# Part of an exponential moved to accumulating DMAs, more of it off ScalarE, and one chunk split in two

## The chip, the cores and the metric

The kernel runs on one core of one Trainium2 chip. A core has five engines that run their own instruction streams and meet through semaphores: TensorE (matrix products, into the eight banks of PSUM), ScalarE (activations), VectorE (elementwise work and reductions), GpSimd, and SyncE, which issues DMAs. GpSimd can issue DMAs too. The metric is device time in microseconds of one execution, as the median of several.

## What is computed

One transformer layer with layer norm ahead of each half, on 2048 rows of 640 columns in bfloat16: attention with 32 heads of 20 columns, then a gated feed-forward of width 1728.

```python
h  = x  + softmax(q k^T * 20**-0.5) v @ wo      # q, k, v = split(layernorm(x) @ wqkv), 32 heads of 20
h2 = h  + (gelu(layernorm(h) @ w_gate) * (layernorm(h) @ w_up)) @ w_down
```

The softmax needs 32 x 2048 x 2048 exponentials, 1,048,576 for each of the 128 partitions. That is the bulk of the work.

## The kernel before

**Tiles, quads, slots, chunks.** Scores are made transposed: a tile is one PSUM bank of 128 keys by 512 columns for one head (where a chunk has 256 queries, the 512 columns are two blocks of keys, with 128 queries four). Four heads are multiplied at once in four row groups of TensorE; a quad is the four tiles of one group of four heads. The queries are cut into chunks (`SIZES`, L316), and each chunk into slots of 64 tiles (16 quads), so that there are 32 slots in all, 2048 tiles. Softmax needs no maximum: a bound for each query is subtracted through an extra row of the product.

**Two ways to the exponential.** Most tiles go through ScalarE: one ACTIVATE takes two or three neighbouring banks and writes bfloat16 into `pts` or `pts2` (18 tiles of room). `D_QUADS` (L334) says how many of a slot's 16 quads go through VectorE instead (`d_exp`, L862 to 902). There each tile is read out of PSUM as scaled int16 (L881), a bit trick that leaves exponent and fraction in one integer; after two tiles (narrow, slots 0 to 17) or four (wide, from slot `D_WIDE` = 18 on) seven instructions in all follow on the whole group: fraction bits out (L892), a linear term (L893), its square (L894), times the fraction (L895), the addition of this correction onto the integer (L896), and a last scaling (L897) after which the bits are the bfloat16 result. (L894 to 896 have two tensor operands, the others one.) `dv0`, `dv` and `dvw` are the buffers of these groups, `df` and `dw` their scratch.

**PSUM patterns.** `PAT` (L818) gives a unit its banks: three and two in turn, or, in the slots of `SIX`, three and three, where a VectorE tile takes the third bank of a unit. The other banks (`BG`, L1210) serve the background: projections, output product, feed-forward. Bank 6 collects the product with v for one slot; its end is the copy to `osb` in `epilogue` (L1029).

**Where the VectorE tiles are placed.** `dq` (L813) gives each a place among ScalarE's tiles: spread over its slot, `D_LEAD` tiles ahead of it; where the lead is 0, the spread is pressed into the first `D_PART` of the slot. The product with v for a VectorE quad is taken up at least `D_LAG` units after its last tile was computed (L1009).

**What sets the order.** A planner (`Sched.schedule`, L94) places all operations by priority, readiness and free banks, with a duration and a latency for each, written in the code; `emit` then writes each engine's instructions in the planned order, with semaphore waits. An engine runs its own list strictly in order. So what the planner took for the time of an operation decides only the order, and an operation that is later than planned holds up all behind it on its engine.

**After a chunk.** `post` (L1065) takes the rows of a finished chunk from `o_nat` through transposes, the product with wo, the residual, the layer norm (`ln_apply`, into `xn_t`, L1101), transposes again (by DMA from SyncE, except in the tail), and the feed-forward as background work (`mms`, L1114; the casts L1155, the gelu pass L1161 on ScalarE with an activation table change on either side, the products L1169; `down`, L1185). `BASE` tells which of four row blocks of `h_sb`, `o_nat`, `hnT` and `ha_f` a chunk uses; a later chunk with the same block waits until the earlier one has left it. `prefetch` (L1055) loads the residual rows. For chunks before the last, the reciprocal root of the layer norm runs on GpSimd (L557 to 590).

Of the kernel before, what the change touches and what calls it, by code (L numbers as in the profile page):

```python
# [7 lines left out]
ALU = mybir.AluOpType  # L8
# [299 lines left out]
D = 640  # L308
# [7 lines left out]
SIZES = (512, 512, 256, 256, 256, 128, 128)  # L316
BASE = (0, 0, 0, 2, 0, 2, 3)
SIX = tuple(range(8, 16))
# [12 lines left out]
D_LAG = 9  # L331
MERGE = ()
PR, PR2 = 12, 6
D_QUADS = (1,) + (2,) * 15 + (2, 2) + (3, 2) * 5 + (2, 2, 2, 2)  # L334
D_FIRST, D_PART = 2, 0.75
D_LEAD = ((0,) * 8, (0, 10, 20) + (24,) * 21)
# [8 lines left out]
def bass_sequential_preLN__mha_block__glu_gated_geglu__prompt_kernel(  # L345
# [12 lines left out]
    with ExitStack() as es:  # L358
# [22 lines left out]
        sel = sb("sel", [128, NA, H])  # L381
        zer = sb("zer", [128, 32])
        sel0 = sb("sel0", [128, 4, 32])
# [17 lines left out]
        osb = sb("osb", [128, 2, 512], FP32)  # L401
        rc = sb("rc", [128, 2, 16], FP32)
        o_nat = sb("o_nat", [128, 4, D])
        sq = sb("sq", [128, 512])
        xn_t = sb("xn_t", [128, 2, D])
        dvx = sb("dvx", [128, 1024])
# [23 lines left out]
        aq = [carve(512) for _ in range(2)] + [sq[:], xn_t[:, 0, 0:512], xn_t[:, 1, 0:512]]  # L430
# [26 lines left out]
        dw1 = carve(1024).bitcast(F16)  # L457
        carve = carver(qt_all[:, 0, :, :].rearrange("p g s -> p (g s)"), NG * 512)
        dvw += [carve(2048).bitcast(I16) for _ in range(2)]
        dv.append(dvx[:].bitcast(I16))  # L460
        zb = dvx[:].rearrange("p (i s) -> p i s", i=2)
        dv0 = [ha_f[:, 1024 * i:1024 * i + 1024].bitcast(I16) for i in range(5)]
        df0, dw0 = ha_f[:, 5120:6144], ha_f[:, 6144:7168].bitcast(F16)
        carve = carver(qt_all[:, 1, :, :].rearrange("p g s -> p (g s)"), NG * 512)
        df2 = carve(2048)
        dw2 = carve(2048).bitcast(F16)
# [42 lines left out]
        cst(I("memset", sel[:], -1.0), "sel", 160)  # L509
        cst(I("affine_select", out=sel[:], in_=sel[:], compare_op=ALU.is_ge, fill=0.0, base=0,  # L510
              pattern=[[128, NA], [-DH, H]], channel_multiplier=1), "sel", 160)
        cst(I("affine_select", out=sel[:], in_=sel[:], compare_op=ALU.is_ge, fill=0.0, base=DH - 1,
              pattern=[[-128, NA], [DH, H]], channel_multiplier=-1), "sel", 160)
        cst(I("memset", sel0[:], 0.0), "sel0")
# [77 lines left out]
        def ln_apply(eng, src, dst, dkey, t, rkeys, prio, first=False):  # L592
            if eng == "act":
                fn = I("activation", dst, src, ACT.Identity, bias=nm[:, t:t + 1], scale=rs[:, t:t + 1])
            else:
# [3 lines left out]
                      reads=list(rkeys) + [("mu", t), ("rs", t)] + ([("nm", t)] if eng == "act" else []), writes=[dkey])  # L599
# [68 lines left out]
        def aqk(t):  # L668
            return ("xn", t - 3) if t >= 3 else ("aq", t)
# [99 lines left out]
        def q_bound0(banks, prio):  # L769
# [3 lines left out]
                bank(bk), sel0[:].rearrange("p j e -> p (j e)"), aq[0], start=True, stop=True),  # L773
# [77 lines left out]
        d_cur = [None]  # L851
        d_late = []
# [9 lines left out]
        def d_exp(b, tile, prio, u):  # L862
# [5 lines left out]
            if h == 0:  # L868
                busy = set(x[1][1] for x in d_done)
                pool = [(kind, i) for i in range(5 if kind != "w" or CHUNKS[slots[units[u][0][0]][0]][0] >= 1536 else 3)]  # L870
                pool = [p for p in pool if p not in busy]
                assert pool
                d_cur[0] = min(pool, key=lambda p: d_last.get(p, -1))
                d_last[d_cur[0]] = len(d_ops)
# [3 lines left out]
            keys = [("dv", i)] + ([("dv", ("l", k)) for k in ((0, 1), (2, 3), ())[i[1]]] if kind == "w" and i[1] < 3 else [])  # L878
            aft = tuple(e_ops) + (q_done(0) if c else ()) + (q_done(1) + tuple(d_late) if kind == "w" else ()) + \
                (q_done(2) if kind == "w" and i[1] > 2 else ())  # L880
# [8 lines left out]
            zi = df.bitcast(I16)  # L889
            w_ = len(d_raw) / 2  # L890
            d = lambda fn, n, r, w: d_ops.append(op("dve", fn, 0.066 + n * w_, prio, reads=r, writes=w))
            d(I("tensor_scalar", zi, v, 511, 2048, ALU.bitwise_and, ALU.bitwise_or), 0.265, [("dv", i)], ["df"])  # L892
            d(I("tensor_scalar", dw, zi, CA / OCT, CB, ALU.mult, ALU.add), 0.265, ["df"], ["dw"])  # L893
            d(I("tensor_tensor", dw, dw, dw, ALU.mult), 0.53, ["dw"], ["dw"])  # L894
            d(I("tensor_tensor", dw, dw, zi, ALU.mult), 0.53, ["df", "dw"], ["dw"])  # L895
            d(I("tensor_tensor", v, v, dw, ALU.add), 0.53, ["dw", ("dv", i)], [("dv", i)])  # L896
# [127 lines left out]
        def epilogue(s_, bk, d_sums):  # L1024
# [4 lines left out]
            op("dve", I("tensor_copy", osb[:, s, :], PS[:, 512 * 6:512 * 7]), c_dve(512), P_QK,  # L1029
               reads=[("O", s_)], writes=[("osb", s)], rel=[bk], after=tuple(d_sums))  # L1030
# [7 lines left out]
            for tt in range(4):  # L1038
                op("pe", lambda eng, tt=tt: eng.transpose(bank(b2)[:, tt * 128:(tt + 1) * 128],
                                                          osb[:, s, tt * 128:(tt + 1) * 128], identf[:]),  # L1040
# [255 lines left out]
```

## Time and profile before

| | |
|---|---|
| runs | 915.77, 915.27, 914.54 us (median 915.27) |
| profiled execution | 916.19 us, span 914.2 us |
| ScalarE busy | 881.1 us (96%) |
| TensorE busy | 824.1 us (90%) |
| VectorE busy | 794.1 us (87%) |
| GpSimd busy | 48.2 us (5%) |
| DMA | 34.33 MB, mean 38 GB/s |

The span is cut where the profiler saw the first and last instruction; the execution's own time is 2.0 us longer. PE is TensorE, PEld its weight loads, DVE VectorE, ACT ScalarE, POOL GpSimd, SP SyncE. Busy time is the time in which at least one instruction of the engine is under way; neighbours may overlap. L366 is the helper through which most instructions are issued, so that groups there are told apart by their tiles: `ps` is PSUM, `rege` and `regw` two large shared regions, `qt_all` the queries, whose finished quarters also serve as VectorE's buffers.

### The profile page before, as it was taken

To read this page: it belongs to the slowest core of one execution; us is meant where nothing else is said; L and a number is where in the kernel's file an instruction comes from. 1 tells how busy PE (TensorE), PEld (TensorE's weight loads), DVE (VectorE), ACT (ScalarE), POOL (GpSimd) and SP (SyncE) were. 2 spreads that over 40 slices of the span, in tenths; PEclk is the share of its full clock that TensorE was granted. 3 is DMA by queue.
4 is the path that set the end of the run, shared out by engine and by line. 5 is a ranking of instruction groups with operands and counts; after the bars stand their busy time and mean duration, and the time that the engine had idled before them with its cause. 6 is when DMAs were issued, how large, how long until landed. Compare 5 with 4: busy or idle time off the path is not lost.

```text
span 914.2 us, 22759 instructions
## 1 busy us (share of the span) xinstructions
PE 824.1 (90%) x9952; PEld 351.2 (38%) x10017; DVE 794.1 (87%) x1458; ACT 881.1 (96%) x789; POOL 48.2 (5%) x149
## 2 busy tenths in 40 slices
PE   3999999999898878899798989999999989998998
PEld 1432322222232222233233333344454445556666
DVE  8869998999899986987899997999998998779753
ACT  7999999999999999999999999999999999999982
POOL 5000000000011000000021000002010000010000
PEclk9999999999999999999999999999999999999999
DMA  7211020323801000000122000000100000110000
GB/s 259 83 31 33 23 62 25 90 67 76 291 25 30 1 1 1 1 8 16 37 35 27 1 1 1 16 30 10 37 16 18 29 1 3 36 27 10 10 17 15
DMA packets 39514, 34.33 MB, mean 38 GB/s; under 512 B 19436, under 2 KB 36936, under 8 KB 39416
## 3 DMA queue, kind: packets, MB, share of 16 engines
q1 hardware_dynamic: 39416, 32.89, 12.9%
q8 instruction: 78, 1.28, 0.6%
q14 instruction: 20, 0.16, 0.1%
HBM read 20.12 MB, written 8.09 MB: 31 GB/s over the span
## 4 chain that ended last, share of the span: by engine, by line
ACT 57%; PE 23%; DVE 17%; POOL 1%; issue 1%; DMA 0%; DVEq 0%
ACT pts L366 36%; ACT rege L366 19%; PE ps L947 6%; DVE qt_all L366 5%; PE ps L366 4%; PE ps L1120 4%; PE ps L663 4%; PE ps L1200 3%; DVE rege L366 3%; DVE qt_all L881 2%; DVE rege L881 2%; DVE rege L1169 1%; DVE rege L1155 1%; ACT L366 1%; DVE regw L701 1%
## 5 line engine op out<-in xcount | busy, mean ns | idle before, releaser
L366 ACT ACTIVATE pts<-ps 128x1024 bf16<-128x1024 f32 (+1 forms) x470 | 561.6, 1349 | 3.6 <-PE ps L947 1.5
L947 PE MATMUL ps<-qt_all,kt_all 32*128 32x256 bf16 (+2 forms) x3584 | 309.2, 289 | 44.8 <-ACT pts L366 22.0
L366 ACT ACTIVATE rege<-ps 128x1024 bf16<-128x1024 f32 (+1 forms) x233 | 288.9, 1342 | 1.9 <-PE ps L366 1.3
L947 PEld LDWEIGHTS ps<-qt_all,kt_all 32*128 32x128 bf16 x3584 | 101.4, 92 | 265.1 <-ACT pts L366 135.6
L366 DVE TENSOR_TENSOR qt_all<-qt_all 128x2048 f16<-128x2048 f16 (+3 forms) x186 | 175.0, 941 | 2.6
L1120 PE MATMUL ps<-rege,regw 128*128 128x256 bf16 (+2 forms) x952 | 151.0, 288 | 12.1 <-ACT rege L366 3.5
L366 PE MATMUL ps<-pts,v_all 128*21 128x256 bf16 (+2 forms) x2070 | 125.4, 291 | 0.4 <-DVE osb L366 0.4
L881 DVE TENSOR_SCALAR qt_all<-ps 128x512 int16<-128x512 f32 x128 | 87.4, 683 | 20.0 <-PE ps L947 19.5
L1120 PEld LDWEIGHTS ps<-rege,regw 128*128 128x128 bf16 x980 | 72.5, 98 | 71.2 <-issue 30.5
L881 DVE TENSOR_SCALAR rege<-ps 128x512 int16<-128x512 f32 x128 | 87.5, 684 | 11.0 <-PE ps L947 10.3
L366 PE MATMUL ps<-rege,v_all 128*21 128x256 bf16 (+2 forms) x1214 | 91.9, 294 | 2.6 <-DVE rege L366 2.3
L663 PE MATMUL ps<-regw 128*128 128x320 bf16 (+1 forms) x340 | 82.5, 353 | 4.2 <-ACT regw L611 1.7
L366 DVE TENSOR_SCALAR qt_all<-qt_all 128x1024 f16<-128x1024 int16 (+2 forms) x153 | 84.0, 557 | 1.9
L1200 PE MATMUL ps<-regw,rege 128*128 128x320 bf16 x448 | 80.6, 302 | 2.0 <-DVE rege L1169 1.0
L366 DVE TENSOR_TENSOR rege<-rege 128x1024 f16<-128x1024 f16 (+1 forms) x90 | 61.4, 683 | 0.8
L366 PEld LDWEIGHTS ps<-pts,v_all 128*21 128x21 bf16 x2070 | 45.1, 91 | 34.8 <-issue 29.3
L1169 DVE TENSOR_TENSOR rege<-rege,ps 128x512 bf16<-128x512 bf16 (+1 forms) x53 | 35.6, 677 | 21.9 <-PE ps L1120 21.8
L1200 PEld LDWEIGHTS ps<-regw,rege 128*128 128x128 bf16 x448 | 36.3, 97 | 34.4 <-issue 16.0
L366 DVE TENSOR_SCALAR rege<-rege 128x1024 int16<-128x1024 int16 (+2 forms) x115 | 48.3, 436 | 0.5
L366 PE MATMUL ps<-kt_all,zer 128*32 128x512 bf16 x560 | 46.9, 384 | 0.0
L663 PEld LDWEIGHTS ps<-regw 128*128 128x128 bf16 x360 | 28.4, 99 | 45.0 <-issue 24.5
L366 PEld LDWEIGHTS ps<-rege,v_all 128*21 128x21 bf16 x1214 | 31.1, 91 | 22.6 <-issue 12.1
(105 smaller groups left out, 587.9 us busy)
## 6 DMA issues: line engine op xcount, KB each, us to landing
rege<-in_A_x_dram SPq DMA_DIRECT2D x6, 640.0 KB, 5.2
q_rows<-regw SPq DMA_DIRECT2D x20, 128.0 KB, 1.7
out_dram<-rege SPq DMA_DIRECT2D x16, 160.0 KB, 2.5
regw<-in_B_w_gate_dram SPq DMA_DIRECT2D x1, 2160.0 KB, 8.4
regw<-in_B_w_up_dram SPq DMA_DIRECT2D x1, 2160.0 KB, 13.4
regw<-in_B_w_down_dram SPq DMA_DIRECT2D x1, 2080.0 KB, 19.8
kt_all<-k_rows SPq DMA_DIRECT2D x12, 160.0 KB
qt_all<-q_rows SPq DMA_DIRECT2D x12, 160.0 KB
```

What stands on the lines that cost most here:

```text
L366: return lambda eng: getattr(eng, method)(*args, **kwargs)
L663: yield op("pe", lambda eng, l=l, r=r, k=k: eng.matmul(bank(bk, n), l, r, start=(k == 0), stop=(k == len(steps) - 1)), c_mm(n) + cold, pri ...
L701: e = op("dve", lambda eng: eng.tensor_copy(dst, bank(bk)), c_dve(512), prio, reads=[key], writes=[dkey], rel=[bk], after=after)
L881: d_ops.append(op("dve", lambda eng: eng.tensor_scalar(v[:, 512 * h:512 * h + 512], bank(b), EXP_MUL, -32000.0, ALU.mult, ALU.max), c_dve( ...
L947: return lambda eng: eng.matmul(out()[:, kk * nq:(kk + 1) * nq], kt_all[32 * j:32 * j + 32, g, kt * 128:(kt + 1) * 128], qt_all[32 * j:32 ...
L1120: op("pe", lambda eng, a=a, f=f, fi=fi: eng.matmul(bank(bk)[:, fi * nq:(fi + 1) * nq], w[:, a, F0[f]:F0[f] + 128], hnT[:, a, 128 * tb:128 ...
L1155: cp.append(op("dve", lambda eng, bg=bg, fv=fv, w=w: eng.tensor_copy(fv, bank(bg, w)), c_dve(w), p, reads=[kg], writes=hkeys(k), rel=[bg], ...
L1169: hdone.append(op("dve", lambda eng, bu=bu, fv=fv, w=w: eng.tensor_tensor(fv, fv, bank(bu, w), ALU.mult), c_dve(w), p, reads=[ku] + hkeys( ...
L1200: op("pe", lambda eng, f=f, o=o, hf=hf, bk=bk: eng.matmul(bank(bk, 320), ha_f[:, o:o + 128], wd[:, f, hf * 320:(hf + 1) * 320], start=(f = ...
```

## The change

Three things, and what they need of memory:

1. In `d_exp`, the addition of the correction is no longer a VectorE instruction. GpSimd issues a DMA from the scratch onto the group's buffer with `accum_op=ALU.add`, on int16, with a semaphore of its own for each buffer. The last scaling on VectorE waits for that semaphore. The planner is given 1.2 us for the issue and 4.0 us (wide) or 2.67 us (narrow) until it has landed. The scratch `dw` is doubled and used in turn, and one more group buffer is added to each kind (six in place of five, four in place of three where one quarter of the queries is still in use).
2. `D_QUADS` sums to 75 in place of 68: slots 18 to 27 have three VectorE quads each (three and two in turn before), slots 28 to 31 three and two in turn (two before). That is seven quads more. Slots from 11 on begin their VectorE tiles 36 tiles ahead (24 before); `D_PART` goes from 0.75 to 0.7 and `D_LAG` from 9 to 8.
3. The second chunk of 512 queries becomes two of 256, in row blocks 0 to 1 and 2 to 3, and the six-bank pattern covers slots 8 to 11 only (8 to 15 before).

To make room, `xn_t` and `sq` go (the layer norm writes back into `o_nat`), `osb` becomes single, and `sel` and `sel0` move into a new region `dwx`.

```diff
-SIZES = (512, 512, 256, 256, 256, 128, 128)
-BASE = (0, 0, 0, 2, 0, 2, 3)
-SIX = tuple(range(8, 16))
+SIZES = (512, 256, 256, 256, 256, 256, 128, 128)
+BASE = (0, 0, 2, 0, 2, 0, 2, 3)
+SIX = tuple(range(8, 12))
...
-D_LAG = 9
+D_LAG = 8
+DA_ISSUE, DA_LAT = 1.2, 4.0
-D_QUADS = (1,) + (2,) * 15 + (2, 2) + (3, 2) * 5 + (2, 2, 2, 2)
-D_FIRST, D_PART = 2, 0.75
-D_LEAD = ((0,) * 8, (0, 10, 20) + (24,) * 21)
+D_QUADS = (1,) + (2,) * 15 + (2, 2) + (3,) * 10 + (3, 2, 3, 2)
+D_FIRST, D_PART = 2, 0.7
+D_LEAD = ((0,) * 8, (0, 10, 20) + (36,) * 21)
...
-        osb = sb("osb", [128, 2, 512], FP32)
+        osb = sb("osb", [128, 512], FP32)
-        sq = sb("sq", [128, 512])
-        xn_t = sb("xn_t", [128, 2, D])
-        dvx = sb("dvx", [128, 1024])
+        dvx = sb("dvx", [128, 2048])
+        dwx = sb("dwx", [128, 2048])
...
             zi = df.bitcast(I16)
+            d_alt[0] += 1
+            a_ = d_alt[0] % len(dw)
+            dk = ("dw", a_)
+            dw = dw[a_]
+            di, dw = dw.bitcast(I16), dw.bitcast(F16)
...
-            d(I("tensor_tensor", dw, dw, zi, ALU.mult), 0.53, ["df", "dw"], ["dw"])
-            d(I("tensor_tensor", v, v, dw, ALU.add), 0.53, ["dw", ("dv", i)], [("dv", i)])
+            d(I("tensor_tensor", di, dw, zi, ALU.mult), 0.53, ["df", dk], [dk])
+            d_ops.append(op(POOL, I("dma_start", v, di, accum_op=ALU.add), DA_ISSUE, prio, reads=[dk], writes=[("dv", i)],
+                            sem="da%s%d" % i, lat=DA_LAT * (w_ + 1) / 3))
             d(I("tensor_scalar", v, v, 0.25, 16256.0 + 128.0 * (CC - 1.0), ALU.mult, ALU.add), 0.265, [("dv", i)], [("dv", i)])
...
-                ln_apply("dve", h_sb[:, tt, :], xn_t[:, t % 2, :], ("xn", t % 2), t, [("h", tt, 0), ("h", tt, 1)], pd)
+                ln_apply("dve", h_sb[:, tt, :], o_nat[:, tt, :], [("on", g, tt) for g in range(NG)], t, [("h", tt, 0), ("h", tt, 1)], pd)
```

## The prediction

> **What bounds the kernel now.** I read the page first, then busy time in stretches, then ScalarE's forms in one stretch and the chain at the gelu passes.
>
> ```profile
> span 914.2 us, 22759 instructions
> PE 824.1 (90%) x9952; PEld 351.2 (38%) x10017; DVE 794.1 (87%) x1458; ACT 881.1 (96%) x789; POOL 48.2 (5%) x149
> ...
> ACT 57%; PE 23%; DVE 17%; POOL 1%; issue 1%; DMA 0%; DVEq 0%
> ```
>
> ScalarE is the fullest engine, yet the chain gives VectorE 17%. Which is it? The stretches:
>
> ```profile
> 60.00:500.00 440.00, 392.33 (x3505) 124.59 (x3545) 393.90 (x785) 438.15 (x379) 17.10 (x57) 1.00 0.16 44
> 500.00:700.00 200.00, 187.75 (x2458) 83.45 (x2470) 189.97 (x291) 198.80 (x173) 10.91 (x28) 1.00 0.06 15
> 700.00:860.00 160.00, 150.15 (x2812) 86.61 (x2809) 135.10 (x211) 158.03 (x138) 7.28 (x28) 0.99 0.08 17
> ```
>
> The columns after the stretch and its length are TensorE, its weight loads, VectorE, ScalarE and GpSimd. ScalarE is busy 99% of every stretch, but its instructions overlap, so a short wait would hide in that. I therefore price one tile. Forms in 100 to 200 us:
>
> ```profile
> L366 ACT ACTIVATE pts<-ps 128x1536 bf16<-128x1536 f32 x30 | 47.7, 1591 | 0.0
> L366 ACT ACTIVATE pts<-ps 128x1024 bf16<-128x1024 f32 x29 | 34.1, 1176 | 0.0
> L366 ACT ACTIVATE rege<-ps 128x1536 bf16<-128x1536 f32 x15 | 24.0, 1598 | 0.1
> L366 ACT ACTIVATE rege<-ps 128x1024 bf16<-128x1024 f32 x15 | 17.7, 1177 | 0.0
> ```
>
> A 1536-column exp holds three tiles, a 1024-column one two: 45 x 3 + 44 x 2 = 223 tiles in 100 us, 0.448 us each. The same count from 350 to 460 us, where units of three are the rule, is 57 x 3 + 38 x 2 = 247 tiles in 110 us, 0.445. All 1776 tiles (370 long, 333 short) need 1776 x 0.448 = 796 us. The first exp starts at 33.3 and the last ends at 881.6: 848 us. Between them lie six gelu passes:
>
> ```profile
> 339.95 1.28 ACT L366
> 341.24 6.46 ACT rege L366 x4
> 347.71 1.28 ACT L366
> 746.66 1.28 ACT L366
> 747.96 3.28 ACT rege L366 x2
> 751.26 1.28 ACT L366
> ```
>
> In this chain a pass of 512 rows costs 9.0 us with its two table loads (two such), one of 256 rows 5.9 (three), the one of 128 about 4.4: 40 us. 848 - 796 - 40 leaves 12 us in which ScalarE waited: it sets the time almost everywhere, and VectorE with 95% of 500 to 700 us comes next.
>
> **The change part by part.**
>
> Fewer exp tiles on ScalarE. D_QUADS sums to 68 before and 75 after: 7 quads, 28 tiles. 28 x 0.448 = 12.5 us off ScalarE's path. Slots 12 to 15 lose the six-bank pattern: 4 x 56 tiles x 0.003 = +0.7.
>
> Second chunk split. One 9.0 us gelu pass becomes two of 5.9: +2.8 us on ScalarE. TensorE gets shorter, more numerous matmuls in slots 8 to 15; its busy share there (about 86%) rises toward that of 256-query slots (91 to 96%, where ScalarE is still at 99%), so nothing on the path. If that cover failed, about 10 us of matmul time (5% of 210 us) would show; a gain below zero is excluded, since no matmul goes away. On the other side the feed-forward of slots 8 to 11 starts when the first chunk's down projection frees h_sb and ha_f (436 us) and no longer waits for slot 15. Half a chunk (14 casts and products at 0.60 us, four 0.48 us sums) is some 10 us of VectorE work; I take 8 of it out of 500 to 700 us, 0 to 10 as ends.
>
> The addition leaves VectorE. Its costliest form, and the pace of VectorE's instructions in order of time:
>
> ```profile
> L366 DVE TENSOR_TENSOR qt_all<-qt_all 128x2048 int16<-128x2048 int16 x24 | 29.1, 1211 | 0.1
> ```
>
> ```profile
> 663.98 0.68 DVE L881 TENSOR_SCALAR qt_all<-ps 128x512 int16<-128x512 f32 x1
> 664.58 1.21 DVE L366 TENSOR_TENSOR qt_all<-qt_all 128x2048 f16<-128x2048 f16 x1
> 665.71 0.25 DVE L1045 RECIPROCAL rc<-ps 128x16 f32<-128x16 f32 x1
> ```
>
> From start to start the wide addition takes 1.13 us and a TENSOR_SCALAR 0.60; a narrow addition, on half the columns, also takes about 0.60. 70 narrow additions (0.60) and 33 wide (1.13) go: 42 + 37 = 79 us. A wide quad costs 4 x 0.60 + 3 x 0.60 + 3 x 1.13 = 7.6 before and 6.5 after, so 7 more add 45. Net 34 us less, but not where VectorE is full: 500 to 700 us held 19 quads (144 us) and will hold about 23 (149 us).
>
> In its place stand 110 accumulating DMAs from GpSimd (70 of 256 KB, 40 of 512 KB), and VectorE's last TENSOR_SCALAR waits for each. Behind it in VectorE's order are the evacuations of VectorE tiles and of the background banks; TensorE waits for those banks, and ScalarE for TensorE. The trace has no such DMA. The order written by the planner leaves 1.2 + 2.67 = 3.9 us for a narrow and 1.2 + 4.0 = 5.2 us for a wide one. The nearest rows, to landing:
>
> ```profile
> k_rows<-rege SPq DMA_DIRECT2D x6, 128.0 KB, 1.8
> rege<-in_A_x_dram SPq DMA_DIRECT2D x3, 320.0 KB, 3.1
> rege<-in_A_x_dram SPq DMA_DIRECT2D x2, 640.0 KB, 4.5
> ```
>
> On that line 256 KB land in 2.6 and 512 KB in 3.9 us: both early. If the accumulation counts the bytes twice, since it also reads its destination, they are 3.9 and 6.0: the wide one is 0.8 late. The Trainium skill (DMA: Bandwidth & Descriptors, Anatomy of one DMA) fits 2.0 us plus bytes over 436 GB/s for a GpSimd-issued DMA: an estimate of 2.6 and 3.2 us; by it nothing is late, the 1.5 us charged below fall away, and the forecast would be 906. No run here shows it yet. To this comes GpSimd's own slowness beside VectorE:
>
> ```profile
> L366 POOL TENSOR_SCALAR sd<-mv x8: 214/234/1197, 266.9 to 843.8; 128x2 bf16<-128x2 bf16 x7, 128x1 bf16<-128x1 bf16 x1
> ```
>
> Minimum, median, maximum: the same tiny operation, with VectorE busy beside it, takes 0.2 us or up to 1.2, so up to 1.0 more per issue. Lateness of a wide DMA thus lies between below zero and 0.8 + 1.0 = 1.8 us. I take 0.3, near the plain-copy rows and the median rows. Cover in 500 to 700 us: 10 us idle, less 5, plus 8: 13 us for 23 DMAs, 0.6 us each. In 700 to 860 us: 25 idle, less 6 slots x 1.4 for the extra quads: 16 us for 17 DMAs, 1.0 each. Narrow ones have 46 idle us in 60 to 500 and 42 more freed, 1.2 us each. So 0.3 is hidden; I charge 1.5 us for waits that hit ScalarE.
>
> The rest: GpSimd's queue also holds the layer norm's reciprocal chains; a DMA among them delays one by about 1.2 us, with VectorE's normalisation, SP's transposes and then the matmuls behind it, which are background with tens of us of room. Leading by 36 tiles finishes a slot's VectorE tiles 12 x 0.448 = 5.4 us earlier, which pays the DMA. In slots 0 to 8, without lead, the last group enters at tile 39 of 56, 7.7 us before the end, against a chain of some 6.8 us; 18 tiles of buffer (8 us) catch a miss. Normalising into o_nat holds it until the transposes at 274 to 282 us; the next writer comes after 269.9, its successor needs osb at 296: hidden by 14 us. SP's queue keeps its transposes and stores for every 128 rows and gains one prefetch (0.4 us). Prologue (33 us) and end (33 us) stay.
>
> Sum: -12.5 + 0.7 + 2.8 + 1.5 = -7.5 us. The profiled execution took 916.19 us (span 914.2 and 2.0 around it), 0.9 above the median 915.27: 908.7 against its own time, 907.8 for the median, which is the forecast.
>
> **The rivals.**
>
> Late landings (slower). Beyond 0.6 us each further us of lateness costs 23 us in 500 to 700, beyond 1.0 another 17 in 700 to 860. At 1.0 us: 9 us, no change; at 1.5 us: 21 + 8 = 29 us, 936; it decides at 1.0 us. For it: the doubled bytes, GpSimd's maxima. Against: its medians, and plain copies.
>
> The port. VectorE's and GpSimd's instructions hold each other off whole, so the freed 79 us come back as waits. By the rows: if an issue is held for one wide TENSOR_SCALAR (0.7 us), on landings that are on time, 23 x 0.1 = 2 us are lost: 906 + 2 = 908. If VectorE is held as long in turn, it is 1.4 us for each DMA, 23 x 0.8 + 17 x 0.4 = 25: 931. For it: GpSimd's maximum lies one VectorE instruction above its minimum. Against: VectorE's own rows show hardly any spread, but GpSimd's operations here are small. The Trainium skill (SBUF — State Buffer, Who interferes with whom) has this rule: a VectorE instruction in a two-port mode and one of GpSimd block each other fully. The spread of GpSimd's row agrees for the one direction; the other is not in this trace.
>
> More relief. If the earlier feed-forward also removes half of the 12 us of ScalarE's waits and the DMAs land early: 907.8 - 1.5 - 6 = 900.
> Nothing gained: the instructions leave VectorE, but its waits for the DMAs, near 1.0 us late, eat what ScalarE gains: 915.
>
> **How the numbers follow.** Forecast 0.52 (902 to 912), relief 0.09 (896 to 902), the port in one direction 0.06 (906 to 912) and in both 0.06 (920 to 935), nothing gained 0.06, late landings 0.21 (917 to 940). 0.2%, 1.8 us, is what a measurement of this kernel can tell from no change (its runs span 0.13%). Faster 0.67, same 0.06, slower 0.27. The range from 899 to 930 leaves out about 0.05 below and 0.12 above.
>
> **What would show it.** ScalarE's exp forms sum to 1748 tiles and its table loads rise from 16 to 18; int16 TENSOR_TENSOR rows gone from VectorE; 110 GpSimd DMAs; a start-to-landing near 4 and 5 us. Wrong: VectorE idle before the int16 TENSOR_SCALAR, released by DMA, above 15 us in 500 to 700; ScalarE under 98% there.

## The result, and the profile after

The changed kernel takes 952.7 us (median of four, 945.8 to 956.2) against 915.5 us for the kernel before on the same chip: a ratio of 1.040, 95% interval 1.037 to 1.043. Slower by 37 us, where the prediction had 7.5 us faster. The profiled execution took 945.76 us, the fastest of the four; the readings below are of that one, 29.6 us above the profiled execution of before (916.19).

From the page of the kernel after: the span, busy time, the software DMA queue (packets, MB, share of 16 DMA engines) and the chain that ended last.

```profile
span 943.7 us, 25161 instructions
PE 847.2 (90%) x11134; PEld 390.2 (41%) x11177; DVE 763.8 (81%) x1426; ACT 875.4 (93%) x785; POOL 148.4 (16%) x259
...
q0 software_dynamic: 15840, 39.33, 23.1%
...
PE 29%; ACT 28%; DVE 25%; DMA 14%; issue 2%; POOL 1%; SPq 0%; POOLq 0%
```

ScalarE and VectorE both do less than before (875 for 881, 764 for 794 us). ScalarE's part of the chain fell from 57% to 28%, and DMA, which was 0%, has 14%. Where? The stretches of before again (TensorE, weight loads, VectorE, ScalarE, GpSimd, granted clock, DMA share, GB/s), with 60 to 500 us also in two parts:

```profile
60.00:500.00 440.00, 386.35 (x4126) 136.70 (x4161) 338.68 (x682) 413.74 (x358) 68.96 (x107) 0.95 0.38 82
500.00:700.00 200.00, 189.98 (x2661) 93.14 (x2655) 185.83 (x304) 198.07 (x173) 30.88 (x51) 1.00 0.37 68
700.00:860.00 160.00, 149.49 (x2619) 83.00 (x2612) 144.93 (x231) 154.18 (x134) 28.32 (x46) 0.98 0.38 72
60.00:270.00 210.00, 186.68 (x1417) 54.11 (x1434) 157.86 (x315) 190.51 (x167) 26.16 (x29) 0.93 0.45 110
270.00:500.00 230.00, 199.67 (x2712) 82.60 (x2733) 180.82 (x367) 223.23 (x192) 42.80 (x78) 0.98 0.31 56
```

The loss is where VectorE has the most room. In 60 to 500 us ScalarE's busy time fell from 438 to 414, in 500 to 700, where VectorE is full and where the prediction looked for danger, only from 198.8 to 198.1. VectorE itself stands idle early: 339 us busy where it was 394, of which the additions taken away explain some 42 (70 at about 0.60).

ScalarE's exponentials, by form, show that the work did go away as announced:

```profile
L367 ACT ACTIVATE pts<-ps 128x1536 bf16<-128x1536 f32 x236 | 350.9, 1498 | 16.6 <-PE ps L959 12.2 <-PE ps L367 3.6
L367 ACT ACTIVATE pts<-ps 128x1024 bf16<-128x1024 f32 x230 | 244.7, 1072 | 9.9 <-PE ps L959 9.8
L367 ACT ACTIVATE rege<-ps 128x1536 bf16<-128x1536 f32 x119 | 177.8, 1502 | 10.2 <-PE ps L959 9.6 <-PE ps L367 0.3
L367 ACT ACTIVATE rege<-ps 128x1024 bf16<-128x1024 f32 x111 | 119.2, 1074 | 3.2 <-PE ps L959 3.2
L367 ACT ACT_TABLE_LOAD x18 | 23.1, 1283 | 1.1 <-PEq L1293 0.8
```

355 long and 341 short ones plus a single tile are 355 x 3 + 341 x 2 + 1 = 1748 tiles, 28 fewer. New is the last column: idle time ahead of the exponentials, ended by TensorE's scores (L959).

From here on I measure ScalarE's waits by its pace. Undisturbed, an exponential of 1536 columns starts 1.331 us after the one before and one of 1024 columns 0.904 us (both from the trace); what lies above that is waiting. Summed over the profiled executions:

```
                    first exp  last exp ends  behind it   waits <270  270-500  >500   TensorE at half clock
before                 33.3        881.6        32.6          5.7       3.2    10.0            3.4 us
after                  32.7        909.9        33.9         29.9      10.6    16.5           54.6 us
```

The account of the 29.5 us between the spans (943.7 and 914.2): -12.2 for the 28 tiles at undisturbed pace (793.5 to 781.3, the single tile counted with 0.48), +2.9 for the additional gelu pass, +38.1 more waits, +1.3 at the end, -0.6 at the start: 29.5.

What TensorE, and through it ScalarE, waited for is in the waits of the kernel after (engine, line, what it waited for: us in total, times, longest), first VectorE's, then ScalarE's and TensorE's:

```profile
DVE rege L367 <- DMA rege<-rege: 25.4, 12, 3.9
DVE qt_all L367 <- DMA qt_all<-qt_all: 8.4, 5, 2.9
DVE rege L367 <- DMA rege<-dwx: 6.8, 4, 1.9
...
ACT pts L367 <- PE ps L959: 22.1, 24, 2.4
ACT rege L367 <- PE ps L959: 12.8, 17, 1.3
...
PE ps L367 <- DVE rege L367: 8.7, 8, 2.6
```

The transfers `rege<-rege` are those of slots 0 to 7. Over all 110 accumulating DMAs VectorE's stops are 25.4 us for the 30 DMAs before 270 us, 14.1 us for the 40 narrow ones after that, 7.3 us for the 40 wide ones. ScalarE's additional waits are 24.2 us before 270, 7.4 to 500 and 6.5 later. Most of the early stops are passed on: without the narrow DMAs (the first run below) ScalarE waits 9.9 us before 270, so that these make some 20 of its 29.9.

One such stop, in the timeline of the kernel after (start, length, engine, what; in brackets the idle time before and what ended it):

```profile
169.53 0.93 POOL L367 DMA_DIRECT2D rege<-rege  x1 [3.06 <-DVE rege L367]
...
172.10 0.29 DVE L367 TENSOR_SCALAR regw<-regw 128x512 int16<-128x512 int16 x1
...
176.29 0.43 DVE L367 TENSOR_SCALAR rege<-rege 128x1024 int16<-128x1024 int16 x1 [3.90 <-DMA rege<-rege]
176.64 0.68 DVE L704 CAST regw<-ps 128x512 bf16<-128x512 f32 x1
176.78 0.40 PE L367 MATMUL ps<-rege,v_all 128*21 128x512 bf16 x4 [2.64 <-DVE rege L367]
177.10 0.79 PE L959 MATMUL ps<-qt_all,kt_all 32*128 32x512 bf16 x3
177.24 0.68 DVE L887 TENSOR_SCALAR rege<-ps 128x512 int16<-128x512 f32 x1
177.53 1.02 ACT L367 ACTIVATE pts<-ps 128x1024 bf16<-128x1024 f32 x1 [1.75 <-PE ps L959]
```

Issued at 169.53, the DMA lands 6.75 us later. VectorE's last scaling has waited for it since 172.39, and behind it in VectorE's list stand a cast (L704) and an evacuation (L887) of PSUM banks. TensorE stops 2.64 us ahead of its product with v, the scores behind that product come late, and ScalarE, which had tiles until 175.8, stands 1.75 us. The late landing went through three engines in 1.3 us.

The landings themselves (KB each, median us from issue to landing):

```profile
rege<-rege POOLq DMA_DIRECT2D x30, 256.0 KB, 3.5
qt_all<-qt_all POOLq DMA_DIRECT2D x12, 512.0 KB, 4.8
```

The medians are within the planner's 3.9 and 5.2 us. The harm is in the spread: of the 30 DMAs of slots 0 to 7, six meet next to no packets of SyncE's queue in their first 3.3 us and land after 3.28 to 3.56 us with no stop at all; eight meet packets worth about 1 us or more of each DMA engine and land after 5.92 to 8.10 us, and these eight make 20.6 of the 25.4 us. SyncE's queue is not the only neighbour. Of all 70 narrow DMAs, the 20 that meet no packet of another queue in that time land after 3.24 to 3.85 us; 12 meet no packet of SyncE's but one of the queue that the page calls `instruction`, and land after 3.25 to 5.11 us. That the other packets delay them is read from this; no run varies these transfers alone.

### The profile page after: what moved, and what is told of

It is laid out like the page before. It is cut to its first block, busy times and chain, and to the rows that moved or that the text cites. A ratio compares the mean times of both kernels' runs of the same rounds, so it can differ in the third digit from the quotient of the medians.

```text
span 943.7 us, 25161 instructions
## 1 busy us (share of the span) xinstructions
PE 847.2 (90%) x11134; PEld 390.2 (41%) x11177; DVE 763.8 (81%) x1426; ACT 875.4 (93%) x785; POOL 148.4 (16%) x259
## 4 chain that ended last, share of the span: by engine, by line
PE 29%; ACT 28%; DVE 25%; DMA 14%; issue 2%; POOL 1%; SPq 0%; POOLq 0%
ACT pts L367 18%; ACT rege L367 9%; PE ps L959 8%; PE ps L367 5%; PE ps L1132 5%; DMA rege<-rege 5%; DVE rege L367 5%; PE ps L666 5%; PE ps L1212 5%; DVE qt_all L367 4%; DVE rege L887 4%; DMA qt_all<-qt_all 3%; DVE dwx L367 3%; DMA rege<-dwx 2%; DVE qt_all L887 2%
## 5 line engine op out<-in xcount | busy, mean ns | idle before, releaser
L367 ACT ACTIVATE pts<-ps 128x1536 bf16<-128x1536 f32 (+1 forms) x467 | 548.9, 1287 | 26.5 <-PE ps L959 22.1
L959 PE MATMUL ps<-qt_all,kt_all 32*128 32x256 bf16 (+2 forms) x4096 | 323.2, 278 | 41.5 <-ACT pts L367 16.5
L367 ACT ACTIVATE rege<-ps 128x1536 bf16<-128x1536 f32 (+1 forms) x230 | 280.1, 1295 | 13.5 <-PE ps L959 12.8
L959 PEld LDWEIGHTS ps<-qt_all,kt_all 32*128 32x128 bf16 x4096 | 111.4, 93 | 254.6 <-ACT pts L367 111.9
L367 PE MATMUL ps<-pts,v_all 128*21 128x256 bf16 (+2 forms) x2328 | 126.9, 280 | 0.8 <-DVE osb L367 0.6
L1132 PEld LDWEIGHTS ps<-rege,regw 128*128 128x128 bf16 x1120 | 86.1, 98 | 64.1 <-issue 29.1
L367 PE MATMUL ps<-rege,v_all 128*21 128x256 bf16 (+2 forms) x1336 | 92.1, 285 | 8.3 <-DVE rege L367 8.0
L887 DVE TENSOR_SCALAR rege<-ps 128x512 int16<-128x512 f32 x120 | 81.9, 684 | 19.0 <-PE ps L959 18.4
L887 DVE TENSOR_SCALAR qt_all<-ps 128x512 int16<-128x512 f32 x124 | 84.7, 683 | 8.8 <-PE ps L959 8.2
L666 PE MATMUL ps<-regw 128*128 128x512 bf16 (+1 forms) x343 | 86.2, 363 | 4.9 <-DMA regw<-in_A_wqkv_dram 1.6
L367 DVE TENSOR_TENSOR qt_all<-qt_all 128x1024 f16<-128x1024 f16 (+1 forms) x80 | 76.1, 951 | 1.1
L367 DVE TENSOR_SCALAR qt_all<-qt_all 128x2048 int16<-128x2048 int16 (+3 forms) x116 | 66.3, 572 | 13.0 <-DMA qt_all<-qt_all 8.4
L367 DVE TENSOR_SCALAR rege<-rege 128x1024 int16<-128x1024 int16 (+2 forms) x112 | 48.8, 438 | 33.7 <-DMA rege<-rege 25.4
L367 PEld LDWEIGHTS ps<-pts,v_all 128*21 128x21 bf16 x2328 | 55.6, 92 | 33.2 <-issue 27.5
L367 POOL DMA_DIRECT2D rege<-rege x30 | 27.4, 913 | 207.7 <-DVE rege L367 203.8
L367 PE MATMUL ps<-kt_all,zer 128*32 128x512 bf16 x580 | 49.7, 391 | 0.0
L367 PEld LDWEIGHTS ps<-rege,v_all 128*21 128x21 bf16 x1336 | 36.5, 91 | 28.5 <-issue 14.2
```

What stands on the lines that cost most here:

```text
L367: return lambda eng: getattr(eng, method)(*args, **kwargs)
L666: yield op("pe", lambda eng, l=l, r=r, k=k: eng.matmul(bank(bk, n), l, r, start=(k == 0), stop=(k == len(steps) - 1)), c_mm(n) + cold, pri ...
L887: d_ops.append(op("dve", lambda eng: eng.tensor_scalar(v[:, 512 * h:512 * h + 512], bank(b), EXP_MUL, -32000.0, ALU.mult, ALU.max), c_dve( ...
L959: return lambda eng: eng.matmul(out()[:, kk * nq:(kk + 1) * nq], kt_all[32 * j:32 * j + 32, g, kt * 128:(kt + 1) * 128], qt_all[32 * j:32 ...
L1132: op("pe", lambda eng, a=a, f=f, fi=fi: eng.matmul(bank(bk)[:, fi * nq:(fi + 1) * nq], w[:, a, F0[f]:F0[f] + 128], hnT[:, a, 128 * tb:128 ...
```

## The experiments

The theory after this reading: **narrow DMAs land late beside SyncE's transfers, VectorE stops for them, and in slots 0 to 17 nothing behind it has slack.** Rivals: the fall of the granted TensorE clock is the cause and not a follower; the wide DMAs or the additional quads overload 500 to 860 us; the split is what costs; the planner's allowance is merely too short. A ratio below is always to the kernel before in the same comparison (914.4 to 915.8 us).

**Wide or narrow alone, and the DMAs alone.** The first two keep all of the change but leave one kind of addition on VectorE:

```diff
-            d_ops.append(op(POOL, I("dma_start", v, di, accum_op=ALU.add), DA_ISSUE, ...
+            if kind == "w":        # second run: kind != "w"
+                d_ops.append(op(POOL, I("dma_start", v, di, accum_op=ALU.add), DA_ISSUE, ...
+            else:
+                d(I("tensor_tensor", v, v, di, ALU.add), 0.53, [dk, ("dv", i)], [("dv", i)])
```

> Only the groups of four tiles (slots 18 to 31, 40 DMAs) keep the accumulating DMA; the 70 groups of two tiles add on VectorE again; chunks, quads and all else as in the changed kernel. Theory A (narrow DMAs that land late beside SyncE's transfers stop VectorE, TensorE idles, its granted clock halves): the stretch of 33 us more of waiting on ScalarE goes with them, mean granted clock back to 0.99 or more, 905 to 912 us. Theory B (the new plan itself, the split and the shorter six-bank stretch, leaves TensorE idle, and the DMAs are innocent): still 940 to 955, clock 0.97. Theory C (GpSimd's issues and VectorE hold each other off at a port): a part proportional to the DMAs taken away, 64% of 37 us, 925 to 932.

> The complement: only the 70 groups of two tiles use the accumulating DMA, the 40 wide groups add on VectorE (1.13 us each, 45 us in all, in slots 18 to 31, where VectorE was already 96% busy with the DMAs). Theory A: the whole loss of the changed kernel stays and the wide additions come on top, 955 to 985 us, clock 0.97 or less. Theory B: 940 to 985 as well, so this run alone does not part A from B. Theory C: 36% of 37 us less, plus the additions: 945 to 975.

The third keeps all DMAs, with chunks, six-bank slots and 68 quads as before:

```diff
-SIZES = (512, 256, 256, 256, 256, 256, 128, 128)
+SIZES = (512, 512, 256, 256, 256, 128, 128)
-SIX = tuple(range(8, 12))
+SIX = tuple(range(8, 16))
-D_QUADS = (1,) + (2,) * 15 + (2, 2) + (3,) * 10 + (3, 2, 3, 2)
+D_QUADS = (1,) + (2,) * 15 + (2, 2) + (3, 2) * 5 + (2, 2, 2, 2)
```

> The kernel before's chunks (second chunk of 512 queries, six-bank slots 8 to 15) and its 68 quads, with the additions by DMA, the lead of 36 and the new buffers: the DMA part alone. Theory A: slower than before by 25 to 40 us (940 to 955), clock 0.97, VectorE waiting for DMAs in slots 0 to 17. Theory B: 905 to 918, clock at 0.99 or more. Theory C: 935 to 950 without a lower clock.

Measured: wide alone 926.7 us, 1.013 (1.011 to 1.015); narrow alone 976.8, 1.067 (1.063 to 1.071); all DMAs with the old chunks and quads 952.4, 1.041 (1.039 to 1.043). VectorE's waits for DMAs, with all DMAs on the old chunks:

```profile
DVE rege L367 <- DMA rege<-rege: 24.8, 13, 4.0
DVE qt_all L367 <- DMA qt_all<-dwx: 8.7, 6, 3.6
DVE qt_all L367 <- DMA qt_all<-qt_all: 5.8, 6, 1.9
```

and with the wide ones alone:

```profile
DVE qt_all L367 <- DMA qt_all<-qt_all: 1.0, 3, 0.5
DVE rege L367 <- DMA rege<-dwx: 0.9, 2, 0.6
```

The narrow DMAs by themselves bring the whole loss, and without them two thirds of it are gone, with ScalarE's waits before 270 us down from 29.9 to 9.9. The rivals "wide DMAs" and "split" fall for the main loss. (Narrow alone is worse than both together, since the 75 quads with their wide additions fill VectorE to 99% in 600 to 700 us: there the wide DMAs do relieve.) The 926.7 us lie outside what the narrow theory had named, 905 to 912, and inside what the port had, 925 to 932, so that the time alone does not part these two; that 30 of the 110 DMAs hold 22 of the 37 us, below, does. And 926.7 us is still 12 us above the kernel before, though its last exponential ends at 876.9, 5 us earlier. That is taken up below.

**Is the clock the cause?** In after TensorE runs at half clock for 54.6 us, in stretches of 3.4 to 13.7 us, against 3.4 us before. More padding work keeps it up:

```diff
-WARM_WIN, WARM_MIN = 3.4, 0.5
-PAD_WIN, PAD_MIN = 3.4, 0.42
+WARM_WIN, WARM_MIN = 3.4, 0.65
+PAD_WIN, PAD_MIN = 3.4, 0.65
```

> The changed kernel with more idle matmuls planned in to keep TensorE busy (the planner's shares PAD_MIN 0.42 and WARM_MIN 0.5 both set to 0.65); nothing else. It asks how much of the loss is the halved clock. If the clock is what turns VectorE's stops of some 45 us into ScalarE's waits: clock 0.985 or more and 920 to 935 us. If the stops alone cost the time and the clock only follows: 940 to 955 whatever the clock does. If padding crowds TensorE: above 955.

951.3 us, 1.040 (1.038 to 1.042): the time at half clock fell from 54.6 to 17.1 us, the mean clock rose from 0.971 to 0.991, and the kernel is no faster. VectorE's waits for DMAs stayed at 48 us. Before 270 us the time at half clock fell from 34 to 17 us, ScalarE's waits only from 29.9 to 27.2; after 270 us they fell by 7 us. But the padding delays the background, and 55.3 us lie behind the last exponential instead of 33.9:

```profile
ACT rege L367 <- DVE rege L1167: 20.0, 2, 15.8
```

So 37 us less at half clock took some 10 us off ScalarE's waits. The run with more room, below, agrees: there half clock is back at 3.4 us without more padding, and 946.4 us remain; its order has waits of its own, so it shows that a full clock does not bring the time back, and not that the half clock cost nothing. The Trainium skill (TensorE: Matmul & The Clock Gate, Terms) prices throttled time at the share of pulses withheld, half of 54.6 us here, an estimate of 27 us; these two runs do not bear that out as a loss of this kernel, since ScalarE's waits before 270 us hardly moved. The clock is not the main cause here; I read it as following the stops.

**Where along the kernel, and would more room help?** The next one leaves the DMAs of slots 0 to 7 on VectorE (`kind != "e"` in the place of `kind == "w"` above); the one after it gives the planner a longer landing time, so that it places the last scaling later:

> The changed kernel with the 30 DMAs of slots 0 to 7 turned back into VectorE additions; the 40 narrow ones of slots 8 to 17 and the 40 wide ones stay. In the changed kernel the late landings (5 to 8 us against 3.3) all but a few fall before 262 us, beside SyncE's row transfers and the three weight loads. Theory A1 (late because other transfers are under way): VectorE's waits for DMAs fall from 46 to below 20 us and the time to 926 to 934, near the 927 of the run with wide DMAs alone. Theory A2 (the narrow chain is too tight in any place): waits near 30 us and 936 to 946.

```diff
-                            sem="da%s%d" % i, lat=DA_LAT * (w_ + 1) / 3))
+                            sem="da%s%d" % i, lat=7.0 if kind != "w" else 5.0))
```

> The changed kernel with all DMAs, but the planner is told 7.0 us for a narrow landing after the issue (2.67 before) and 5.0 for a wide one (4.0), so that more of VectorE's other work is written between a DMA and the instruction that waits for it. If the waits of VectorE are the loss: waits under 12 us, 926 to 936. If the DMAs cost in another way (the port, the traffic itself): 942 to 955 with few waits. If the longer chains starve the product with v: ScalarE waits at slot ends, 945 or more.

Without the first 30 DMAs: 929.3 us, 1.015 (1.013 to 1.018), ScalarE's waits before 270 us 9.9. So these 30 cost some 22 of the 37 us; in proportion to their number, as the port would have it, they would cost 10. With more room: 946.4 us, 1.034 (1.032 to 1.037). VectorE's waits for DMAs fell to 8.4 us and the clock rose to 0.998 (3.4 us at half), yet ScalarE's waits before 270 stayed at 31.5 us, with another releaser:

```profile
ACT pts L367 <- PE ps L367: 22.1, 8, 5.0
ACT rege L367 <- PE ps L367: 13.5, 3, 8.4
```

L367 on TensorE is the product with v. A scaling that is placed later hands its tiles over later, and a slot's last product with v then ends behind its last exponential: the chain no longer fits before the slot's end. (Of ScalarE's stops the long ones, 2.5 to 8.4 us, come some 30 us apart, about one for each slot. The time fits the port's expectation too, 942 to 955 with few waits for DMAs; this releaser does not.) The stop is not an error of one number in the planner; the DMA lengthens a chain that, in slots without a lead, has no room for it.

**What holds the runs without narrow DMAs?** In the run with wide DMAs alone the last exponentials end early, and then ScalarE still has a gelu pass of 256 rows to do:

```profile
874.01 2.92 ACT L367 ACTIVATE pts<-ps 128x1536 bf16<-128x1536 f32 x3
876.95 1.28 ACT L367 ACT_TABLE_LOAD   x1
...
879.76 3.28 ACT L367 ACTIVATE rege<-rege 128x2048 bf16<-128x2048 bf16 x2
```

In the kernel before, that pass lies among the exponentials, and behind the last one only the 128-row pass is left:

```profile
880.12 1.48 ACT L366 ACTIVATE pts<-ps 128x1536 bf16<-128x1536 f32 x1
881.61 1.28 ACT L366 ACT_TABLE_LOAD   x1
...
885.75 1.70 ACT L366 ACTIVATE rege<-rege 128x1792 bf16<-128x1792 bf16 x1 [1.33 <-DVE rege L1155]
```

The background work of a chunk has come late: 46.7 us lie behind the last exponential instead of 32.6. Which engine delays it? Four runs: wide DMAs with the old chunks; the new chunks with all additions on VectorE and 68 quads; wide DMAs with gate and up summed over two of five column blocks for all but the last chunk (three fifths of these matmuls left out); wide DMAs with the squaring (L905) left out of the wide groups. For the third, the kernel before with the same cut as a control.

```diff
-                    for a in range(NA):
+                    n_a = NA if tail else 2
+                    for a in range(n_a):
```

```diff
+            if kind != "w":
                 d(I("tensor_tensor", dw, dw, dw, ALU.mult), 0.53, [dk], [dk])
```

> As the run with wide DMAs alone (927 us, of which 47 us lie behind the last exp, 33 in the kernel before), but with the second chunk in one piece of 512 queries and six-bank slots 8 to 15. If the split's extra matmuls (11256 against 9952) fill TensorE and push the feed-forward into the end: end back to 33 to 37 us, 906 to 915. If the end comes of the shorter exp phase itself, since the background work then has less time: end still 43 to 48 us, 920 to 930.

> The split and the new buffers and leads alone: 68 quads, all additions on VectorE. If the split costs by TensorE: 922 to 932, with 40 us or more behind the last exp. If it is worth nothing or a gain, as its second gelu pass (2.8 us) is all that is on the path: 912 to 919.

> The run with wide DMAs alone (927 us, 47 of them behind the last exp), with TensorE's background work cut: for all chunks but the last, the gate and up products sum over two of the five blocks of 128 inputs, so those results are incomplete. That takes some 45 us of matmuls out of 844. If TensorE's fill holds the end (theory T): the end falls to 32 to 37 us and the time to 903 to 913. If VectorE's order holds it (theory V): end above 42, 920 or more.

> The run with wide DMAs alone, with VectorE's work cut by about as much: the squaring in the 40 wide groups is left out (1.13 us each, 45 us; the exponentials of those tiles are wrong). Theory V: end 32 to 37 us, 903 to 913. Theory T: end above 42 us, 918 to 928.

> The control: the kernel before with the same cut of the gate and up products (two of five input blocks for all chunks but the last). ScalarE sets its time, so little should come of it: 908 to 915. If TensorE co-decides in the kernel before already, 895 to 907.

```
run                                    us     ratio (95%)              last exp ends  behind it
wide DMAs, new chunks, 75 quads       926.7   1.013 (1.011 to 1.015)      876.9        46.7
 the first, old chunks                926.5   1.012 (1.010 to 1.015)      875.3        49.0
 the first, less for TensorE          919.5   1.007 (1.004 to 1.010)      890.1        27.3
 the first, less for VectorE          915.3   1.001 (0.999 to 1.002)      881.8        31.5
new chunks, no DMA, 68 quads          922.1   1.008 (1.005 to 1.011)      896.4        30.5
before, less for TensorE              923.9   1.010 (1.008 to 1.012)      896.0        25.8
```

The last two columns are of the profiled execution; in the run without DMAs that one took 928.9 us, 6.9 above the median. The split makes no difference (926.7 and 926.5), and the run without DMAs fell between its two expectations (922 us, but no long end). Less VectorE work brings the end back and gives 11 us; less TensorE work brings the end back too, but the exponentials then end 13 us later. The control shows the same: taking matmuls away from the kernel before makes it *slower* by 9 us, with half clock for 34 instead of 3.4 us. Its stretches from 500 us on:

```profile
500.00:700.00 200.00, 179.48 (x2422) 76.45 (x2431) 184.02 (x278) 193.06 (x167) 4.85 (x14) 0.96 0.06 14
700.00:860.00 160.00, 140.93 (x2668) 71.68 (x2678) 138.94 (x217) 157.77 (x138) 9.33 (x28) 0.99 0.07 18
```

TensorE is busy 179 us in place of 188, at a clock of 0.96 in place of 1.00, and ScalarE falls from 198.8 to 193.1. So the runs with less TensorE work say little about the end; the one with less VectorE work speaks for VectorE's quads as what delays the background.

**The order's parameters.** All runs so far carry `D_LAG` 8, `D_PART` 0.7 and the lead of 36, which I had not priced. Wide DMAs with the old values:

```diff
-D_LAG = 8
+D_LAG = 9
-D_FIRST, D_PART = 2, 0.7
-D_LEAD = ((0,) * 8, (0, 10, 20) + (36,) * 21)
+D_FIRST, D_PART = 2, 0.75
+D_LEAD = ((0,) * 8, (0, 10, 20) + (24,) * 21)
```

> The run with wide DMAs alone (927 us) with the lead of 24, D_PART 0.75 and D_LAG 9 of the kernel before. If the new leads cost (a slot's product with v and its queries come later in the order, one wait of 5.6 us near 143 us that all runs with the new values show): 918 to 924, that wait gone. If they are needed to pay the DMA: 928 to 940, with ScalarE waiting at slot ends after 500 us.

923.0 us, 1.010 (1.007 to 1.012): some 3.6 us better. One stop of ScalarE, 5.6 us at 138 to 144 us, is in every run that has the new `D_LAG` and `D_PART` and its early additions on VectorE, and gone here.

This run and two below (the room alone, and the wide DMAs with it) have a fault in common. With the lead of 24 beside the new buffers, the first two evacuations of a wide group of slot 18 are written over two narrow tiles of slot 17 that the product with v has still to read. So these three compute 2 of the 2048 tiles wrong and are no usable kernels. No instruction is missing or added by it, and it happens once, in slots 17 to 18, far behind the stop at 138 to 144 us; but no run here shows what it does to the time.

**Is it the quads?** Wide DMAs, old chunks and 68 quads; then with the old `D_LAG` and `D_PART`; then with 71 quads (the expectation says 72; 71 is what the list sums to, 12 tiles).

> The wide additions alone on accumulating DMAs; the additions of narrow groups on VectorE; chunks of 512, 512, 256, 256, 256, 128, 128 and 68 quads as before, the planner's parameters of after. This is a pure relief of VectorE by some 33 wide additions of 1.13 us. Theory A (the end behind the last exp is long only where more quads fill VectorE): the end comes back to 33 us or below, and the time is 908 to 914. Theory B (the after kernel's parameters for the order cost by themselves, the wait near 143 us among them): 915 to 922, with over 8 us of ScalarE's waits before 270 us. Theory C (a landing of a wide DMA stops VectorE where it is full): 915 to 922, with VectorE's waits for DMA above 8 us.

> As the run with 68 quads and wide additions alone on DMAs, with D_LAG 9 and D_PART 0.75 as in the kernel before; the lead of 36 tiles stays. Theory A and theory C: within 3 us of that run. Theory B: 4 to 8 us faster than that run, and the wait of 5.6 us near 143 us is gone.

> As the run with D_LAG 9 and D_PART 0.75, with 72 quads instead of 68: 16 exp tiles fewer on ScalarE (7 us) against four more quads of 6.5 us on VectorE, in the slots from 18 on. If VectorE has room for them: 5 to 7 us faster than the run with 68 quads. If the end behind the last exp is VectorE's to set there: no faster, with the last exp some 5 us earlier and the end longer by as much.

931.6 us, 1.018 (1.016 to 1.020); 924.7, 1.011 (1.008 to 1.014); 924.1, 1.010 (1.007 to 1.013). The first is a miss: with the quads taken out, the end did come back to 36.0 us, but the time went *up* by 5 us, since the 28 tiles are on ScalarE again. With the new parameters the additional quads are worth having (931.6 against 926.5 with 75); with the old `D_LAG` and `D_PART` three more gave 0.6 us, within the spread. The old `D_LAG` and `D_PART` gave 6.9 us, and the stop at 138 to 144 us is gone although the lead of 36 stays: it is one of these two, or both, and not the lead. The wide DMAs, which take 33 additions off VectorE, gained nothing. So the last three runs take the rest of the change apart:

> All additions on VectorE, the chunks, the 68 quads, D_LAG, D_PART and the lead of 24 tiles as in the kernel before. What is left of the change is the room made for the DMAs: the normalised rows go to o_nat, one osb instead of two, more and other buffers for the quads. If this room costs nothing: within 2 us of the kernel before. If holding o_nat or the single osb delays the work around a slot's end (the prediction called it hidden by 14 us): 3 to 10 us slower, and then that explains most of what the runs with wide DMAs and 68 quads lost.

> As the run with the room alone, with D_LAG 8, D_PART 0.7 and the lead of 36 tiles. If these parameters of the order cost by themselves: 4 to 8 us slower than the run with the room alone, with ScalarE's wait of 5.6 us near 143 us. If not: within 2 us of it.

> The wide additions on DMAs, everything else as in the run with the room alone. Against that run it shows what 33 wide additions off VectorE are worth. Pure relief: 1 to 6 us faster than it. If a slack VectorE is worth nothing, since ScalarE sets the time: within 2 us. If the order around a DMA or the granted clock costs: 3 to 10 us slower, with the half clock in more than 15 us of the span.

Measured: the room for the DMAs alone (`o_nat`, one `osb`, more buffers; old chunks, quads and parameters, all additions on VectorE) 917.4 us, 1.002 (1.001 to 1.003); with the new parameters 925.9, 1.011 (1.008 to 1.014); with the wide DMAs and the old parameters 926.4, 1.012 (1.010 to 1.014). ScalarE's first waits with the new parameters, and VectorE's waits for DMAs with the wide DMAs:

```profile
ACT dvx L1153 <- PE ps L1131: 12.3, 4, 7.9
ACT pts L367 <- PE ps L958: 6.7, 3, 5.7
```

```profile
DVE rege L367 <- DMA rege<-dwx: 6.4, 5, 2.8
DVE qt_all L367 <- DMA qt_all<-dwx: 5.5, 2, 3.1
DVE dvx L367 <- DMA dvx<-qt_all: 2.0, 2, 1.6
DVE qt_all L367 <- DMA qt_all<-qt_all: 1.4, 2, 0.7
```

The 5.7 us stop near 143 us belongs to the new parameters, without any DMA. And the expected pure relief falls: 33 wide additions off VectorE cost about 9 us over the run with the room alone. (Both have the fault named above, so it does not part them.) VectorE is less busy in 500 to 700 us (170.6 us, against 187.0 with the additions on it), but ScalarE is no busier (194.4 against 195.8), and VectorE stops 15.3 us for landings. In the profiled executions these two differ by 3.4 us, nearly all of it ScalarE's waits behind 500 us (15.7 against 11.8); the rest of the 9 us appears only in the other executions, at a lower mean clock, and no run here separates it further. (The profiled one was at half clock for 6.8 us, not for the 15 that I had tied to such a loss.)

Put in order, each rung one part more than the one above it (ratios, so that they can be compared across comparisons):

```
room for the DMAs alone                       1.002
+ lead 36, D_LAG 8, D_PART 0.7                1.011
+ wide additions on DMAs                      1.018
+ narrow additions on DMAs                    1.041
+ second chunk split, six banks 8-11, 75 quads  1.040
```

Of the 37 us the narrow DMAs take about 21, the parameters 8, the wide DMAs 6, the buffers 2; the quads and the split together bring back about one in that company, and no run shows why no more. Another order of adding gives other parts: with the old parameters the wide DMAs cost 9 instead of 6. The first rung is one of the three runs with two wrong tiles. No version was faster than the kernel before; the one without the squaring, which leaves work out, only equals it.

## Why the prediction was wrong

- **Right: what ScalarE saves.** -12.5 us for 28 tiles at 0.448, measured -12.2. +2.8 for the additional gelu pass, measured +2.9. 1748 tiles, 18 table loads and 110 GpSimd DMAs as named. ScalarE at 99% in 500 to 700 us. One reading behind it was off without touching the sum: of the six gelu passes of before only five (35.8 us) lie between the first and the last exponential, the one of 128 rows lies behind. So ScalarE's waits there were 18.9 us by its pace, and not 12.
- **The step that failed: "Narrow ones have 46 idle us in 60 to 500 and 42 more freed, 1.2 us each. So 0.3 is hidden".** The mean stop for a narrow DMA was 39.5 us / 70 = 0.56 us, well under 1.2 us; as an average the cover was there. But the eight late ones before 270 us stopped VectorE for 1.2 to 3.9 us each, and VectorE's idle time elsewhere in the stretch can't be drawn on: VectorE works its list in order, and with the scaling the evacuations and casts behind it wait. Idle time is cover only if it lies directly behind the waiting instruction, or if what comes next is not needed at once. The prediction named this queue and then priced it by a sum over 440 us. It charged 1.5 us for waits that hit ScalarE; ScalarE waited 38.1 us more, some 20 of them before 270 us through the narrow DMAs.
- **Landing times.** The ends were 2.6 to 3.9 us for 256 KB and 3.9 to 6.0 for 512 KB. Undisturbed, 3.3 and 4.5 us were measured: inside both. But for the narrow ones I took only rows of stretches with little else on the DMA engines as bounds, though the stretch shown of before has a DMA share of 0.16 in 60 to 500 us, two to three times the 0.06 and 0.08 behind it (0.25 in 60 to 270). Beside SyncE's transfers they took up to 8.1 us. The Trainium skill (DMA: Bandwidth & Descriptors, Anatomy of one DMA) gives an estimate of 2.6 and 3.2 us; the trace puts these 0.7 and 1.3 us higher even undisturbed, and that formula has no term for other traffic, beside which the eight late ones came to 5.9 to 8.1 us. By it nothing would have been late; the measurement decides.
- **"the last group enters at tile 39 of 56, 7.7 us before the end, against a chain of some 6.8 us; 18 tiles of buffer (8 us) catch a miss".** It failed with the landings: a DMA of 7 us makes that chain some 10 us. The run with more room showed it directly, with 22.1 + 13.5 us of ScalarE waiting for the product with v.
- **"Leading by 36 tiles finishes a slot's VectorE tiles ... 5.4 us earlier, which pays the DMA".** The lead of 36 begins in slot 11, behind most of the loss, and the new parameters cost about 8 us by themselves; `D_LAG` and `D_PART` alone cost 6.9 beside the wide DMAs. These two were not priced at all: a term put at nothing without a reason.
- **The rival "late landings"** had the right mechanism and sign, but the wrong place (500 to 860 us, wide DMAs, decided at 1.0 us of mean lateness). There the wide DMAs made VectorE stop 7.3 us in all.
- **"The port" did not show.** GpSimd's issue took 0.86 us undisturbed, 0.87 to 1.00 in the mean of its groups; VectorE's fast rows kept their durations (the main group of TENSOR_SCALAR on 2048 columns: mean 0.677 us before, 0.680 after). The rule of the Trainium skill (SBUF — State Buffer, Who interferes with whom) fits the issues that took up to 1.6 us, but a stop of VectorE's side large enough to matter is not in this trace.
- **The split as "nothing on the path"** holds: 926.7 with, 926.5 without. **"Prologue (33 us) and end (33 us) stay"** held for the kernel after (32.7 and 33.9), but by luck: its last exponential came 33 us later than with wide DMAs alone, where the end was 47 us, which the runs with 68 quads (36.0 us) and with less VectorE work (31.5) put down to VectorE's additional quads.

The signs named as proof of the contrary (VectorE's DMA waits above 15 us, ScalarE under 98%) were right in kind and pointed at the wrong stretch.

## What to carry to other kernels

Moving an instruction from an in-order engine to a DMA replaces 0.6 us of work by a round trip of 3 to 8 us in the middle of a dependent chain; price it by the *latest* landing beside the other traffic of that stretch and by what stands directly behind the waiting instruction, never by the engine's idle time averaged over a stretch. Freed time on an engine that doesn't set the end need not be worth anything: here taking 33 wide additions off VectorE cost 6 to 9 us. And where an order was written by a planner for given latencies, its parameters belong on the list of what has to be priced.

## What the runs showed that I had not expected

- Taking TensorE work away made the kernel slower: 923.9 against 914.5 us, with the granted clock at half for 34 us instead of 3.4. The stretches at half clock come in pieces of about 3.4 us and its multiples (3.4, 6.8, 10.2, 13.7 in after). That TensorE's short idle times bring them on is how I read it; the padding run fits, but no run varies that alone.
- One order of instructions took different times with the granted clock: the run with the room and the new parameters had spans of 920.3 us at a mean clock of 0.998 and of 927.7 at 0.985 to 0.987. Bringing the clock back (0.971 to 0.991 and 0.998) nevertheless didn't restore the time of after.
- An accumulating DMA within SBUF lands after 3.3 us for 256 KB and 4.5 us for 512 KB when it is alone, and took up to 8.1 us beside SyncE's transfers.
